# Turned tokens read back by one transfer a tile, and the last block's sums gated earlier

## The chip, the cores and the metric

The kernel runs on one core of a Trainium2 chip. The metric is the device time of one execution in microseconds (us); the kernel before takes 471.35 us, the median of three runs (470.61 to 472.19). The five engines of the core are TensorE (PE; PEld is its weight load), VectorE (DVE), ScalarE (ACT), GpSimd (POOL) and SyncE (SP), which here issues nearly all transfers. Sixteen DMA engines carry the transfers.

## The reference

One transformer-like layer on 2048 tokens of 448 features, conditioned on a vector `c`:

```python
mod = (silu(c) @ w_mod)              # six rows of 448: sa, ca, ga, sb, cb, gb
h = layernorm(x) * (1 + ca) + sa
x = x + ga * ssm_conv(h)             # long convolution along the tokens, plus h * Dskip
h = layernorm(x) * (1 + cb) + sb
x = x + gb * ((silu(h @ w_gate) * (h @ w_up)) @ w_down)   # 448 -> 1792 -> 448
```

## The kernel before

The 2048 tokens are 16 tiles of 128; two tiles make a block, so there are eight blocks. The hidden width 1792 is 14 slices of 128 (`f` = 0 to 13). Per block and slice, TensorE computes gate and up (`gate_up`, 21 steps of contraction 64, the gate's on the upper half of the array and the up's on the lower), VectorE and ScalarE form silu(gate) * up and split it into a high and a low part (`gating`, lines L774 to L792; in the last slice L774, then L781 to L784 in two halves), and TensorE adds the slice's part of the down product to two PSUM banks, `sums` (`point`, called in the middle of a later slice's steps: after the number of steps given by `POINT`). All matrix products are made as three products of high and low parts. The weights are loaded and split in the first block and stay in SBUF.

While TensorE works on block b, the other engines prepare the two tiles of block b + 1: first norm, the convolution (by a short path of triangular products, which lands in the sums of the other PSUM pair), second norm. What is done in which slice is written by hand in `PLANS`: one string for the first block, one for the blocks 1 to 6, one for the last; a `;` ends a slice, a letter is a step and the digit its tile. The steps that matter here:

- `X`, `Y`: second norm, two VectorE operations (L207, L209). A `+` before a name puts the step inside `gating`, after the product silu * up (L786) and ahead of the split into high (L791, ScalarE) and low (L792, VectorE); without it the step follows the gating.
- `T` (`turn`): VectorE transposes the tile in blocks of 32 x 32 (L239), and SP writes it to DRAM (`xd`, L240).
- `U` (`turned_back`): SP reads it back from DRAM into `place[q]` (L245), so that the features stand on the partitions, the 64 features of a chunk twice (both halves of the array need them).
- `split_turned`: at the block's last slice ScalarE (L252) and VectorE (L253) split the turned tokens into `hhi` and `hlo`, chunks 0 to 3 ahead of the last gating and 4 to 6 behind it. TensorE's first products of the next block read these.

In `turned_back` four transfers of 32 partitions each, four runs of 224 numbers a partition, bring a tile back. SP works its list in order: each write, each wait and each read is issued after the one before it.

In the last block nothing is prepared. After slice 13's gating, `last_sums` multiplies the two finished sums (of slices 0 to 11) by the row `gb` (L832) and adds them to `x` (L833), and `finish` computes the down products of slices 12 and 13 (whose weights were multiplied by `gb` before), adds them in three parts (L852) and issues the output transfers.

Of the kernel before, what the change touches and what calls it, by code (L numbers as in the profile page):

```python
# [10 lines left out]
F32 = mybir.dt.float32  # L11
# [3 lines left out]
OP = mybir.AluOpType  # L15
# [3 lines left out]
L, D, N, F = 2048, 448, 256, 1792  # L19
# [4 lines left out]
NF = F // 128  # L24
# [9 lines left out]
PLANS = (  # L34
    """pre: s0 t0 R0 ; mid: f ; g a0 s1 t1 R1 ; b0 G ; r0 h0 ; +v0 a1 c0 ; A0 p0 b1 ; B0 e0 E0 ; r1 h1 u0 w0 M0 ; +v1 X0 Y0 c1 p1 ; A1 T0 ;
    B1 E1 m1 M1 ; U0 X1 Y1 T1 ; U1 e1 ; L0 ; L1""",
    """n0 n1 N ; +l0 a0 b0 k0 ; +l1 k1 r0 h0 ; +v0 a1 b1 c0 ; A0 p0 ; B0 e0 E0 c1 ; r1 h1 m0 M0 p1 ; +v1 X0 Y0 L0 L1 ; A1 T0 U0 ; B1 E1 m1 M1 ; X1 Y1 T1 U1 ; e1 ; ;""",
    "; l0 k0 ; l1 k1",
)
POINT = ([12] + [20] * 12 + [12], [12] + [18] * 12 + [12])  # L40
ORDER = """sf x0 x1 sc m10 se sd m11 m20 m21 m00 m01 sb sa m40 m41 m30 m31 w0 m50 m51 w1 d0 d1 x2 w2 x3 d2"""

PLAN = """t4 pa0 t1 S1 t2 pa1 t3 wi ca gp S20 wr h00 gpc gt h01 mp S21 gac m0 dg gdm mpc k0 a2 t5 sq1 mk gdr h10 cp S3 v00 dga a3 o00
# [8 lines left out]
def f32(ap):  # L52
    return ap.bitcast(F32)
# [3 lines left out]
def tile_kernel(ctx, tc, x, a_re, a_im, b_re, b_im, c_re, c_im, log_dt,  # L57
                wd, wgate_up, states, groups, vecs, dft, idft, out):
    nc = tc.nc
    sy, ve, sc, po, pe = nc.sync, nc.vector, nc.scalar, nc.gpsimd, nc.tensor  # L60
# [5 lines left out]
    dram = ctx.enter_context(tc.tile_pool(name="dram", bufs=1, space=bass.MemoryType.DRAM))  # L66
# [9 lines left out]
    xs = {}  # L76
    xbuf = [const.tile([128, D], F32, name=f"x{q}") for q in range(4)]
    gb = const.tile([128, D], F32)
# [18 lines left out]
    place = [stages_[:, q].rearrange("p k c -> p (k c)") for q in (2, 0)]  # L97
# [13 lines left out]
    def split_d(j, part=None):  # L111
        hi, lo = wp[j]
        if not part:
            sc.copy(hi, wdn[j])
        if part != 0:
            ve.tensor_tensor(lo, wdn[j], f32(hi), op=OP.subtract)

    def split_w(j, part):
        w = raw[j]
        if part == 0:  # L120
            sc.copy(wgu[j][:, 0], w)  # L121
        else:
            ve.tensor_tensor(wgu[j][:, 1], w, f32(wgu[j][:, 0]), op=OP.subtract)  # L123
# [69 lines left out]
    n1, n2 = Norm("a"), Norm("b")  # L193
# [37 lines left out]
        ve.tensor_scalar(i, j, 0.0, None, op0=OP.is_equal)  # L231
        return i

    xd = [dram.tile([128, D], F32, name=f"xd{q}") for q in range(2)]

    def turn(i, q):

        src, dst = h_of(i), v0_of(i)
        ve.transpose(dst.rearrange("p (b k r) -> p k b r", b=2, k=7), src.rearrange("p (k b c) -> p k b c", b=2, k=7))  # L239
        sy.dma_start(xd[q], dst)  # L240

    def turned_back(q):
        for z in range(4):
            b = z % 2
            sy.dma_start(place[q][z * 32:(z + 1) * 32].rearrange("c (a n) -> c a n", a=4),  # L245
                         xd[q][:, b * 224:(b + 1) * 224].rearrange("(a c) n -> c a n", a=4))

    def split_turned(ks):
        for q in range(2):
            src = turned[q].rearrange("p a k r -> p k a r")[:, ks]  # L250
            hi, lo = (h[:, ks, cols(q)].rearrange("p k (a r) -> p k a r", a=4) for h in (hhi, hlo))
            sc.copy(hi, src)  # L252
            ve.tensor_tensor(lo, src, f32(hi), op=OP.subtract)  # L253
# [40 lines left out]
    with tc.tile_pool(name="pre", bufs=1) as pre:  # L294
# [4 lines left out]
        for kind, q in ((n[0], n[1:]) for n in ORDER.split()):  # L299
# [3 lines left out]
            elif kind == "m":  # L303
                g, b = int(q[0]), (slice(0, 2 * D), slice(2 * D, NM))[int(q[1])]
# [36 lines left out]
        for z in range(2):  # L341
# [16 lines left out]
        m0, m0_, a1, a2, m1 = (pre.tile([128, 4], F32, name=q) for q in ("m0", "m0_", "a1", "a2", "m1"))  # L358
# [3 lines left out]
        h01, v0, v1, hd = ([pre.tile([128, w], t, name=f"{n}_{q}") for q in range(2)] for n, t, w in  # L362
                               (("h", F32, D), ("v0", F32, D), ("v1", F32R, D), ("hd", F32, D)))
# [116 lines left out]
        k0, k1 = CV[:, 0:D], DN[2][:, 0:D]  # L480
# [259 lines left out]
    def run_blocks(pools, stages, first=None):  # L740
# [3 lines left out]
        def both(top, low):  # L744

            done = []
            for pair in zip_longest(top, low):
                for e, op in zip(halves, pair):
                    if op:
                        o, w, r, start, stop = op  # L750
                        done.append(pe.matmul(o, w[e], r[e], start=start, stop=stop).ins)  # L751
            return done

        def ffn(b, ts, fresh, last, todo):
            n, sums = 256, SUMS[b % 2]
            pp = {}

            def gate_up(f):
                w, ps = wgu[f], [bank(), bank()]
                prod = [(0, hhi), (1, hhi), (0, hlo)]  # L760
                if fresh and f < NF - 1:
                    order = [(z, k) for z in ((0, 1, 2) if f == 0 else (0, 2, 1)) for k in range(7)]
                else:
                    order = [(z, k) for ks in (LOW, HIGH) for z in range(3) for k in range(7)[ks]]
                ops = [(w[:, prod[z][0], k], prod[z][1][:, k], q == 0, q == 20) for q, (z, k) in enumerate(order)]
                return ps, [[(t[:, 0:n], *o) for t in ps] for o in ops]

            def gating(f, ps, nw):
                p = hid.tile([128, 256], F32, name="p") if fresh else p_of[f % 2]
                hi = hid.tile([128, 256], F32R, name="phi")  # L770
                lo = hid.tile([128, 256], F32R, name="plo")
                for g, a in todo.get(-2, []) if f == 0 else []:
                    g(*a)
                gate_ready[:] = [sc.activation(p, ps[0][:, 0:n], AF.Silu).ins.name]  # L774
                pp[f] = hi, lo
                if f == NF - 1:
                    if fresh:
                        split_d(f, 1)
                    for q in range(3):
                        for o in [cols(q)] * (q < 2):  # L780
                            ve.tensor_tensor(p[:, o], p[:, o], ps[1][:, o], op=OP.mult)  # L781
                            sc.copy(hi[:, o], p[:, o])
                        for o in [cols(q - 1)] * (q > 0):
                            ve.tensor_tensor(lo[:, o], p[:, o], f32(hi[:, o]), op=OP.subtract)  # L784
                    return
                ve.tensor_tensor(ps[1][:, 0:n], p, ps[1][:, 0:n], op=OP.mult)  # L786
                if fresh:
                    split_d(f, 1)
                for g, a in todo.get((f, "+"), []) + todo.get(-1, [])[f * NF:]:
                    g(*a)  # L790
                sc.copy(hi, ps[1][:, 0:n])  # L791
                ve.tensor_tensor(lo, ps[1][:, 0:n], f32(hi), op=OP.subtract)  # L792
                if nw is not None:
                    split_w(nw, 0)
                if fresh:
                    sc.copy(wp[f + 1][0], wdn[f + 1])
# [25 lines left out]
            def gated(f):  # L822

                raw = stage_d[NS - 1]
                sy.dma_start(raw, wd[f * 128:(f + 1) * 128, :])
                po.tensor_tensor(raw, raw, gb, op=OP.mult)
                wdn[f] = raw

            def last_sums():

                for q, i in enumerate(ts):
                    ve.tensor_tensor(sums[q][:, 0:D], sums[q][:, 0:D], gb, op=OP.mult)  # L832
                    ve.tensor_tensor(xs[i], sums[q][:, 0:D], xs[i], op=OP.add)  # L833

            def finish():
                o = [*SUMS[1 - b % 2], bank()]
# [36 lines left out]
            for f in range(NF):  # L873
                ps, ops = gate_up(f)
                ops = list(zip(*ops))
                at = POINT[b > 0][f]
                both(ops[0][:at], ops[1][:at])
                point(f)
                both(ops[0][at:], ops[1][at:])
                if f == NF - 1 and not last:  # L880
                    split_turned(LOW)
                gating(f, ps, f + 2 if fresh and f + 2 < NF else None)
                if f == NF - 1 and not last:
                    split_turned(HIGH)
                if last and f in (2, 5):
                    gated(NF - 2 + (f == 5))
                if last and f in (4, 7):
                    split_d(NF - 2 + (f == 7))
                if last and f == NF - 1:
                    last_sums()  # L890
                    return finish()
                if fresh and f == 0 and first is None:
                    sy.dma_start(run[0:1], run[127:128])
                for g, a in todo.get(f, []):
                    g(*a)
                if fresh:
                    if f + 2 < NF:
                        split_w(f + 2, 1)
                    pools.load(f + 2 + NS, f + NS)
# [4 lines left out]
        if first is not None:  # L904
# [8 lines left out]
            for q, i in enumerate(TILES[0]):  # L913
                t = work.tile([128, 7, 2, 64], F32, name="xn2")
# [156 lines left out]
    for i in TILES[-1]:  # L1071
        c = slice(256 if i + 1 == NT else 0, D)
# [33 lines left out]
def build(nc, aps, out):  # L1106
    with tile.TileContext(nc) as tc:
        a = dict(aps)
        tile_kernel(tc, a["A_u"].rearrange("b l d -> (b l) d"), *[a[n] for n in _INS[1:] + ["B_w_gate_up", "A_states", "w_mod_groups", "c_log_dt", "dft", "idft"]],
                    out.rearrange("b l d -> (b l) d"))  # L1110
# [20 lines left out]
```

## Time and profile before

| | |
|---|---|
| median of three runs | 471.35 us (470.61 to 472.19) |
| the profiled execution's own time | 470.57 us |
| its span (first to last instruction) | 468.8 us |
| mean granted TensorE clock | 0.997 |
| turned tokens written to DRAM (L240) | 14 transfers of 224 KB, median 1.9 us to landing |
| turned tokens read back (L245) | 56 transfers of 112 KB, median 3.1 us to landing |
| gate and up weights loaded (L104) | 14 transfers of 448 KB, median 3.4 us to landing |

The page's first part gives the busy time of each engine and its share of the span. A wait is a line "engine tile line <- engine tile line: us in total, times, longest": who stood idle, and what released it. The chain of waits is followed back from the last instruction: at each step to what released it. A timeline row has the start in us, the duration, engine, line, operation, output<-input, and in brackets the idle time just before. "SPq" is the queue of SyncE: its rows are the issue of a transfer, not the transfer. The DMA view gives, for a stretch, the packets, the megabytes and the share of the sixteen engines' time by queue: q1 is SP's queue, q10 ScalarE's.

### The profile page before, as it was taken

To read this page: it belongs to the slowest core of one execution; us is meant where nothing else is said; L and a number is where in the kernel's file an instruction comes from. 1 tells how busy PE (TensorE), PEld (TensorE's weight loads), DVE (VectorE), ACT (ScalarE), POOL (GpSimd) and SP (SyncE) were. 2 spreads that over 40 slices of the span, in tenths; PEclk is the share of its full clock that TensorE was granted. 3 is DMA by queue.
4 is the path that set the end of the run, shared out by engine and by line. 5 is a ranking of instruction groups with operands and counts; after the bars stand their busy time and mean duration, and the time that the engine had idled before them with its cause. 6 is when DMAs were issued, how large, how long until landed. Compare 5 with 4: busy or idle time off the path is not lost.

```text
span 468.8 us, 14329 instructions
## 1 busy us (share of the span) xinstructions
PE 445.5 (95%) x6271; PEld 422.9 (90%) x6271; DVE 296.0 (63%) x605; ACT 159.8 (34%) x390; POOL 95.6 (20%) x125
## 2 busy tenths in 40 slices
PE   6889998899999999999999999999998999999993
PEld 4558988799999999999998999999998999999993
DVE  4888979865765756565764756565764756543224
ACT  5876564532323222332223232332223232322220
POOL 1235112015200241025100241025100241001000
PEclk9999999999999999999999999999999999999998
DMA  8963555502021202202021202202021102211001
GB/s 303 406 235 100 178 161 174 140 22 82 2 80 42 63 19 60 62 12 70 2 80 43 78 3 60 62 20 63 2 80 42 41 3 60 61 40 44 3 3 45
DMA packets 22408, 35.71 MB, mean 76 GB/s; under 512 B 3008, under 2 KB 18240, under 8 KB 22336
## 3 DMA queue, kind: packets, MB, share of 16 engines
q1 hardware_dynamic: 21696, 34.53, 22.8%
q8 instruction: 51, 0.84, 0.8%
q10 hardware_dynamic: 640, 0.18, 0.2%
q14 instruction: 21, 0.17, 0.1%
HBM read 27.76 MB, written 6.88 MB: 74 GB/s over the span
## 4 chain that ended last, share of the span: by engine, by line
PE 69%; DVE 11%; DMA 7%; ACT 6%; issue 4%; SPq 2%; POOL 1%; DVEq 0%; ACTq 0%; POOLq 0%
PE bank L751 43%; PE dn L751 16%; PE cv L751 8%; DMA raw<-xd 3%; DMA xd<-m 3%; SPq L245 2%; DVE gu L123 2%; DVE bank L786 1%; DVE m L207 1%; DVE m L209 1%; ACT gu L121 1%; DVE m L239 1%; ACT phi L791 1%; ACT hhi L252 1%; DVE plo L792 1%
## 5 line engine op out<-in xcount | busy, mean ns | idle before, releaser
L751 PE MATMUL bank<-hhi,gu 64*128 64x256 f32 x3136 | 225.4, 275 | 7.8 <-DVE gu L123 3.9
L751 PEld LDWEIGHTS bank<-hhi,gu 64*128 64x128 f32 x3136 | 205.3, 184 | 11.3 <-DVE gu L123 5.1
L751 PE MATMUL bank<-hlo,gu 64*128 64x256 f32 x1568 | 131.8, 274 | 0.0
L751 PEld LDWEIGHTS bank<-hlo,gu 64*128 64x128 f32 x1568 | 119.2, 184 | 1.8
L786 DVE TENSOR_TENSOR bank<-raw,bank 128x256 f32<-128x256 f32 x91 | 39.0, 429 | 102.3 <-ACT raw L774 101.7
L774 ACT ACTIVATE raw<-bank 128x256 f32<-128x256 f32 x98 | 37.6, 384 | 188.3 <-PE bank L751 188.3
L751 PE MATMUL dn<-wdh,plo 64*128 64x448 f32 x332 | 84.2, 362 | 1.3 <-DVE plo L792 1.3
L751 PE MATMUL dn<-wdh,phi 64*128 64x448 f32 x332 | 84.2, 360 | 0.3 <-DVE run L727 0.3
L751 PE MATMUL dn<-wdl,phi 64*128 64x448 f32 x332 | 84.0, 360 | 0.0
L792 DVE TENSOR_TENSOR plo<-bank,phi 128x256 fp32r<-128x256 f32 x104 | 44.0, 423 | 29.5 <-ACT phi L791 29.5
L791 ACT CAST phi<-bank 128x256 fp32r<-128x256 f32 x104 | 38.9, 374 | 61.9 <-DVE bank L786 61.9
L751 PEld LDWEIGHTS dn<-wdh,plo 64*128 64x128 f32 x332 | 44.9, 184 | 3.3 <-DVE plo L792 1.8
L751 PEld LDWEIGHTS dn<-wdh,phi 64*128 64x128 f32 x332 | 44.9, 184 | 1.8 <-DVE run L727 0.6
L751 PEld LDWEIGHTS dn<-wdl,phi 64*128 64x128 f32 x332 | 45.0, 184 | 1.0
L751 PE MATMUL cv<-wdh,plo 64*128 64x448 f32 x108 | 38.8, 360 | 0.0
L751 PE MATMUL cv<-wdl,phi 64*128 64x448 f32 x108 | 38.8, 359 | 0.0
L751 PE MATMUL cv<-wdh,phi 64*128 64x448 f32 x108 | 38.6, 358 | 0.0
L183 POOL TENSOR_SCALAR rsa<-mva 128x2 f32<-128x2 f32 (+1 forms) x9 | 3.5, 387 | 112.4 <-DVE mva L155 111.8
L183 POOL TENSOR_SCALAR rsb<-mvb 128x1 f32<-128x1 f32 x16 | 4.3, 266 | 104.0 <-DVE mvb L155 103.4
L253 DVE TENSOR_TENSOR hlo<-raw,hhi 128x512 fp32r<-128x512 f32 (+1 forms) x28 | 16.8, 624 | 11.7 <-ACT hhi L252 10.3
L970 POOL TENSOR_TENSOR m<-m,gm 128x448 f32<-128x448 f32 x12 | 13.9, 1158 | 44.7 <-issue 37.3
L751 PEld LDWEIGHTS cv<-wdh,plo 64*128 64x128 f32 x108 | 19.9, 184 | 0.6
(237 smaller groups left out, 533.5 us busy)
## 6 DMA issues: line engine op xcount, KB each, us to landing
raw<-in_B_w_gate_up_dram SPq DMA_DIRECT2D x14, 448.0 KB, 3.4
raw<-xd SPq DMA_DIRECT2D x56, 112.0 KB, 3.1
rawd<-in_B_w_down_dram SPq DMA_DIRECT2D x16, 224.0 KB, 3.6
xd<-m SPq DMA_DIRECT2D x14, 224.0 KB, 1.9
x<-in_A_u_dram SPq DMA_DIRECT2D x12, 224.0 KB, 3.6
out_dram<-x SPq DMA_DIRECT2D x11, 224.0 KB, 2.5
wm<-in_w_mod_groups_dram SPq DMA_DIRECT2D x5, 448.0 KB, 8.2
wm<-in_w_mod_groups_dram SPq DMA_DIRECT2D x5, 336.0 KB, 8.2
```

What stands on the lines that cost most here:

```text
L121: sc.copy(wgu[j][:, 0], w)
L123: ve.tensor_tensor(wgu[j][:, 1], w, f32(wgu[j][:, 0]), op=OP.subtract)
L183: po.tensor_scalar(rs[:, 0:n], self.mv[:, 0:n, 1], EPS, None, op0=OP.add)
L207: ve.scalar_tensor_tensor(to, xs[i], m, cbw, op0=OP.subtract, op1=OP.mult)
L245: sy.dma_start(place[q][z * 32:(z + 1) * 32].rearrange("c (a n) -> c a n", a=4), xd[q][:, b * 224:(b + 1) * 224].rearrange("(a c) n -> c a ...
L253: ve.tensor_tensor(lo, src, f32(hi), op=OP.subtract)
L751: done.append(pe.matmul(o, w[e], r[e], start=start, stop=stop).ins)
L774: gate_ready[:] = [sc.activation(p, ps[0][:, 0:n], AF.Silu).ins.name]
L786: ve.tensor_tensor(ps[1][:, 0:n], p, ps[1][:, 0:n], op=OP.mult)
L791: sc.copy(hi, ps[1][:, 0:n])
L792: ve.tensor_tensor(lo, ps[1][:, 0:n], f32(hi), op=OP.subtract)
L970: en.tensor_tensor(v, h, g, op=OP.mult)
```

## The change

Four edits:

1. `turn` writes a tile by two transfers instead of one. The DRAM buffer is now 64 rows of 896 numbers, laid out as the features-on-partitions tile will be: feature, then group of 32 tokens, then the 224 numbers of a run. Each transfer has 128 runs of 896 bytes.
2. `turned_back` reads a tile by one transfer instead of four: the 64 rows of 3584 bytes, twice, onto the 128 partitions.
3. In the blocks 1 to 6 the second tile's `X` goes into the gating of its slice (`+X1`).
4. In the last block, slice 13's `point` comes after 8 steps instead of 12, and three of the four operations of `last_sums` (the first tile's two, and the second's multiplication) stand ahead of slice 13's gating; the fourth stays behind it.

```diff
-    """n0 n1 N ; ... ; B1 E1 m1 M1 ; X1 Y1 T1 U1 ; e1 ; ;""",
+    """n0 n1 N ; ... ; B1 E1 m1 M1 ; +X1 Y1 T1 U1 ; e1 ; ;""",
...
-POINT = ([12] + [20] * 12 + [12], [12] + [18] * 12 + [12])
+POINT = ([12] + [20] * 12 + [12], [12] + [18] * 12 + [12], [12] + [18] * 12 + [8])
...
-    xd = [dram.tile([128, D], F32, name=f"xd{q}") for q in range(2)]
+    xd = [dram.tile([64, 2 * D], F32, name=f"xd{q}") for q in range(2)]
...
-        sy.dma_start(xd[q], dst)
+        for k in range(2):
+            sy.dma_start(xd[q][k * 32:(k + 1) * 32].rearrange("c (a n) -> a c n", a=4), dst[:, k * 224:(k + 1) * 224])
...
     def turned_back(q):
-        for z in range(4):
-            b = z % 2
-            sy.dma_start(place[q][z * 32:(z + 1) * 32].rearrange("c (a n) -> c a n", a=4),
-                         xd[q][:, b * 224:(b + 1) * 224].rearrange("(a c) n -> c a n", a=4))
+        sy.dma_start(place[q], xd[q][None].to_broadcast([2, 64, 2 * D]))
...
-            def last_sums():
-
-                for q, i in enumerate(ts):
-                    ve.tensor_tensor(sums[q][:, 0:D], sums[q][:, 0:D], gb, op=OP.mult)
-                    ve.tensor_tensor(xs[i], sums[q][:, 0:D], xs[i], op=OP.add)
+            def last_sums(*parts):
+
+                for q, k in parts:
+                    i, t = ts[q], sums[q][:, 0:D]
+                    if k == 0:
+                        ve.tensor_tensor(t, t, gb, op=OP.mult)
+                    else:
+                        ve.tensor_tensor(xs[i], t, xs[i], op=OP.add)
...
-                at = POINT[b > 0][f]
+                at = POINT[2 if last else b > 0][f]
...
+                if last and f == NF - 1:
+                    last_sums((0, 0), (0, 1), (1, 0))
                 gating(f, ps, f + 2 if fresh and f + 2 < NF else None)
...
                 if last and f == NF - 1:
-                    last_sums()
+                    last_sums((1, 1))
                     return finish()
```

More of the change, by code (lines that the diff above doesn't have):

```diff
@@ L36 @@
     B1 E1 m1 M1 ; U0 X1 Y1 T1 ; U1 e1 ; L0 ; L1""",
-    """n0 n1 N ; +l0 a0 b0 k0 ; +l1 k1 r0 h0 ; +v0 a1 b1 c0 ; A0 p0 ; B0 e0 E0 c1 ; r1 h1 m0 M0 p1 ; +v1 X0 Y0 L0 L1 ; A1 T0 U0 ; B1 E1 m1 M1 ; X1 Y1 T1 U1 ; e1 ; ;""",
+    """n0 n1 N ; +l0 a0 b0 k0 ; +l1 k1 r0 h0 ; +v0 a1 b1 c0 ; A0 p0 ; B0 e0 E0 c1 ; r1 h1 m0 M0 p1 ; +v1 X0 Y0 L0 L1 ; A1 T0 U0 ; B1 E1 m1 M1 ; +X1 Y1 T1 U1 ; e1 ; ;""",
     "; l0 k0 ; l1 k1",
 )
-POINT = ([12] + [20] * 12 + [12], [12] + [18] * 12 + [12])
+POINT = ([12] + [20] * 12 + [12], [12] + [18] * 12 + [12], [12] + [18] * 12 + [8])
 ORDER = """sf x0 x1 sc m10 se sd m11 m20 m21 m00 m01 sb sa m40 m41 m30 m31 w0 m50 m51 w1 d0 d1 x2 w2 x3 d2"""
```

## The prediction

> **What bounds the kernel now.** I read the page's engine line first, then the chain that ended last.
>
> ```profile
> PE 445.5 (95%) x6271; PEld 422.9 (90%) x6271; DVE 296.0 (63%) x605; ACT 159.8 (34%) x390; POOL 95.6 (20%) x125
> ...
> PE 69%; DVE 11%; DMA 7%; ACT 6%; issue 4%; SPq 2%; POOL 1%; DVEq 0%; ACTq 0%; POOLq 0%
> ```
>
> TensorE is the bound. Anything off TensorE counts only where TensorE waits for it. The list of waits says where the turned tokens make it wait:
>
> ```profile
> ACT hhi L252 <- DMA raw<-xd: 10.2, 6, 2.4
> ...
> PE bank L751 <- ACT hhi L252: 3.4, 5, 1.2
> ```
>
> So the transfers that the change touches cost 3.4 us of TensorE's time, in five of the seven block boundaries. No more than that can be won there. The chain around one boundary (between the third and the fourth block) shows how that comes about. Columns: start, duration, what.
>
> ```profile
> 187.82 0.44 DVE bank L786
> ...
> 188.69 0.42 DVE plo L792
> 189.12 0.60 DVE m L207
> ...
> 189.81 0.69 DVE m L209
> ...
> 190.53 0.66 DVE m L239
> ...
> 191.24 1.93 DMA xd<-m
> ...
> 193.23 0.30 SPq L245
> ...
> 194.79 3.04 DMA raw<-xd
> ...
> 197.85 0.63 ACT hhi L252
> ...
> 198.52 1.54 PE bank L751 x21
> ```
>
> The second tile is normalised (L207, L209), turned (L239), written out (1.93 us) and read back by four transfers, from the first issue at 193.23 to the last landing at 197.83: 4.6 us. TensorE resumes at 198.52. The timeline gives what it lost, and the first tile's transfers of the same block (issue start, us in issue):
>
> ```profile
> 182.35 0.33 SPq L240 DMA_DIRECT2D xd<-m  x1
> 184.35 1.75 SPq L245 DMA_DIRECT2D raw<-xd  x4
> ...
> 198.52 1.20 PE L751 MATMUL bank<-hhi,gu 64*128 64x256 f32 x16 [0.34 <-ACT hhi L252]
> ```
>
> So TensorE had run out of work at 198.52 - 0.34 = 198.18. That is this boundary's deadline.
>
> **The earlier normalisation (+X1).** L207 moves from behind the low half L792 to the front of it. It can start at 188.26, when L786 ends, takes 0.68 with its gap, and L792 follows at 188.95 instead of 188.69, ending at 189.37. L209 starts at 189.40, not 189.81: the second tile's write is issued 0.41 us earlier, at 190.83. The low half comes 0.26 us later; it is used only by the next slice's down products, some 3 us on, so that costs nothing.
>
> **The transfers.** Bytes stay: 224 KB out and 448 KB back per tile. Runs change. The write becomes two transfers of 128 runs of 896 bytes, the read one of 128 runs of 3584 bytes. SP issues three transfers in place of five; a write's issue takes 0.33 us, so the second is issued some 0.35 us behind the first, and the read waits for both. What decides is how many of the 16 DMA engines share a transfer. The DMA view over 243 to 252 us (one boundary: one write, four reads, one copied row) and over 10 to 20 us (engines saturated):
>
> ```profile
> DMA  0000008980000009554662100026987300000100
> ...
> q1 hardware_dynamic: 720, 0.69, 26.1%
> ...
> q10 hardware_dynamic: 32, 0.00, 0.3%
> ```
>
> ```profile
> DMA packets 1418, 4.07 MB, mean 407 GB/s; under 512 B 159, under 2 KB 159, under 8 KB 1418
> ```
>
> Five transfers of 128 runs are 640 packets; the other 80 are 16 for each transfer. Every engine closes its own share, so all 16 took part. Even the single row (q10, 3.5 KB) makes 32: 16 pieces and 16 closings, so it was cut into 16 to be spread. In all transfers of this program the outermost step of both sides counts 128, 32 or 16. The new read's source counts 2 outermost (the same 64 rows twice), the new write's target counts 4 (the four groups of 32 tokens). No row shows such a transfer, so the cost has two ends.
>
> *Wide end:* spread over 16 as now. The weight load is the nearest row, same bytes, same runs, same target:
>
> ```profile
> DMA to landing us min/median/max: 3.1/3.4/9.7
> ```
>
> Then both writes land at about 190.83 + 0.35 + 1.93 = 193.1, the read at 196.5, and its split (0.63) ends at 197.2, a microsecond before the deadline. The boundaries' 3.4 us go, and no other wait is near: the split's own products follow in the order of today.
>
> *Narrow end:* the engines share the outermost step, two for the read and four for the writes. Saturated, 16 engines moved 407 GB/s, 25.4 GB/s each: a 3584-byte run takes 0.141 us. Each of two engines gets 64 runs, 9.0 us, where eight runs now take 1.1; with the 2.0 us that the 3.1 of the load hold beside its eight runs, a read takes 11.0 us. Short runs: 26.1% of 16 engines over 9 us for 720 packets is 0.052 us each. Each of four engines gets 32 runs of each of two writes, 3.3 us, where nine packets now take 0.47 of the 1.93: the pair lands 4.8 us after its first issue.
>
> I take the narrow end. In every row the closings equal a divisor of the outermost counts, and the copied row had to be given 16 pieces for it; a scheme blind to the nesting would not need that. The Trainium skill, "DMA: Bandwidth & Descriptors", section "Rules for kernel authors", says it outright: "an outermost dim of size c < 16 — e.g. a leading zero-stride broadcast of c copies — confines the whole DMA to at most c engines". By that rule the sum is the narrow one, 578; without it 465.6; no transfer of this trace has such a dim, so the trace can neither agree nor disagree.
>
> *Working, narrow, at this boundary.* When data begin after an issue:
>
> ```profile
> 243.51 0.34 SPq L240 DMA_DIRECT2D xd<-m  x1
> ```
>
> First tile: write at 182.35, landed 187.15, read issued 187.2; its data run on two engines from 188.05 to 197.05 (data begin 0.84 us after an issue: in the DMA row above, in slices of 0.225 us from 243, the first busy slice starts at 244.35, and the write was issued at 243.51; the rest of the fixed part comes behind the data). Second tile: writes issued at 190.83, but two of their four engines are still at the first tile's read, in the same queue; they finish at 197.05 + 3.33 = 200.4, landed 201.0 (1.93 - 0.84 - 0.47 = 0.62 behind the last run). Read issued 201.05, landed 212.05, split 212.7, TensorE resumes at 212.75 against the deadline of 198.18: 14.6 us. If the queue does not hold the second tile's writes back, they land at 195.65, the read at 206.7, TensorE resumes at 207.4: 9.2 us, the lower bound. At 20.2 GB/s an engine (the page's whole queue below) a run takes 0.177, two reads 4.7 us more in all: the upper bound, 19.3.
>
> ```profile
> q1 hardware_dynamic: 21696, 34.53, 22.8%
> ```
>
> (22.8% of 16 x 468.8 is 1710 us for 34.53 MB.) The other five steady boundaries run the same order of work, and I give them the same price. The first boundary keeps its order (no +X1 there):
>
> ```profile
> 81.92 1.76 SPq L245 DMA_DIRECT2D raw<-xd  x4
> 85.19 0.34 SPq L240 DMA_DIRECT2D xd<-m  x1
> ...
> 93.88 1.07 PE L751 MATMUL bank<-hhi,gu 64*128 64x256 f32 x16
> ```
>
> First read's data 82.8 to 91.8, second writes landed 95.75, read landed 106.8, TensorE resumes at 107.5 instead of 93.88: 13.6 us (7.8 without the queue). Sum: 6 x 14.6 + 13.6 = 101.2, less the 3.4 already paid: 97.8 us.
>
> *Who stands behind the waits.* On ScalarE the split of the second tile stands ahead of the last slice's SiLU, so that slice's gating waits with it, as today. On SP the next transfers are the block's output writes, due two slices later; they are not missed. In the first block a W_down slice's load queues behind the first read on two engines; what it delays falls into the stall.
>
> *TensorE after a pause.* It never pauses over 2 us now, save at the start. There:
>
> ```profile
> 1.52 4.97 PE L291 MATMUL bank<-tri 128*128 128x512 f32 x14 [1.52 <-DVE tri L323]
> ...
> 155.59 1.21 PE dn L751 x12
> ```
>
> In steady state 12 products of 448 columns take 1.21, two at a time, so 512 columns cost 0.23 and 14 of them 3.2; the first ones took 4.97. A pause of 14 us may cost up to those 1.7 us each time: between 0 and 12 for seven; I take 12, the only row of TensorE that starts from rest.
>
> **The end.** The chain there:
>
> ```profile
> 457.73 1.08 PE bank L751 x18
> ...
> 458.86 0.39 ACT raw L774
> ...
> 459.27 0.30 DVE raw L781
> ...
> 459.93 0.49 DVE plo L784 x2
> 460.42 0.56 DVE dn L832
> ...
> 461.00 0.62 DVE x L833
> 461.62 0.55 DVE cv L832
> ...
> 462.20 0.62 DVE x L833
> ...
> 463.27 0.68 DVE x L852 x2
> ```
>
> Three of the four operations L832/L833 move ahead of the last gating. They need the finished sums, which four steps (eight products, 0.46 us) fewer ahead of the point bring to 457.3, and VectorE, which is free at 457.57 (row below). They take 1.76 (460.42 to 462.18), to about 459.4, while SiLU L774 ends at 459.25: the gating slips 0.13. Then one operation of 0.62 and the three additions (1.13): 462.35 instead of 463.95, with TensorE's last product done at 461.51 + 0.13. Gain 1.6 us; at worst the slip takes all 1.76 and 0.1 is left.
>
> ```profile
> 457.15 0.42 DVE L792 TENSOR_TENSOR plo<-bank,phi 128x256 fp32r<-128x256 f32 x1 [0.44 <-ACT phi L791]
> ...
> 461.24 0.27 PE L845 MATMUL bank<-wdh,plo 128*128 128x192 f32 x1
> ```
>
> **Sum.** The profiled execution took 470.57 (span 468.8 and 1.8 around it), 0.8 below the median 471.35. 470.57 + 97.8 + 12 - 1.6 = 578.8; I say 578. Own range: without queue and without the slow start 470.57 + (6 x 9.2 + 7.8 - 3.4) - 1.6 = 528; with slower runs, partly, 600.
>
> **Rivals.**
> *Wide spread:* the engines share the 128 runs however nested. 470.57 - 3.4 - 1.6 = 465.6, faster. For it: the 128 partitions are the outermost count on the other side. Against it: the copied row's 16 pieces. It decides if a read closes with 16 packets, not 2.
> *Narrow writes, wide read:* the pair lands at 4.8 instead of 1.93, 0.41 earlier issued: +2.4; the read takes 3.35 instead of 4.6: -1.25. Six boundaries x 1.15 - 1.6 = +5.3: 475.9, slower.
> *Wide, but the turn isn't worth it:* two writes of short runs and the wait for both eat what the read saves, about 470; same. Against it: a microsecond of slack above.
>
> **Chances.** Narrow read 0.68, narrow writes alone 0.05, wide 0.22, no change 0.05. So slower 0.73, faster 0.22, same 0.05 (0.3%, 1.4 us, is about what tells from no change here: the runs span 470.61 to 472.19). The narrow case's own range leaves out three in ten, so the stated range reaches to the wide case: 464.5 to 600.
>
> **What would show it.** Right: the packets of a boundary's read are 128 + 2, the writes' 128 + 4; the read lands 10 to 12 us after its issue, not 3; the wait of TensorE for the split is 9 to 15 us seven times, also at the first boundary; the DMA share between blocks is 1 to 2 tenths for long. The end: one L833 behind the gating, last addition about 1.6 us nearer to TensorE's last product. Wrong: 16 closings each, a landing near 3.3 us, no TensorE wait for the split, and a time near 465.6.

## The result, and the profile after

The changed kernel takes 587.19 us (median of four runs, 585.71 to 589.51) against 471.34 us: a ratio of 1.246, 95% interval 1.242 to 1.251. The profiled execution took 587.11 us with a span of 585.3, so 116.5 us more span than before. The page of the changed kernel, engine line and chain:

```profile
PE 461.8 (79%) x6271; PEld 441.1 (75%) x6271; DVE 295.0 (50%) x605; ACT 160.2 (27%) x390; POOL 95.6 (16%) x125
...
PE 59%; DMA 27%; DVE 7%; ACT 3%; issue 3%; SPq 1%; POOL 1%; ACTq 0%; DVEq 0%; POOLq 0%
```

TensorE does the same 6271 products. Its share falls from 95% to 79%, and DMA holds 27% of the chain instead of 7%. The waits name the place (us in total, times, longest):

```profile
ACT hhi L250 <- DMA raw<-xd: 108.4, 13, 13.7
...
PE bank L749 <- ACT hhi L250: 107.3, 7, 15.9
```

TensorE's wait for the split (the second line) was 3.4 us in all, in five boundaries; now it is 15.3 on average, in all seven. The chain around the boundary between the third and the fourth block, the one shown before (line numbers are those of the new text: the turned tile's write is L241, its read L244, the split L250):

```profile
225.13 0.66 DVE m L239
...
226.44 9.89 DMA xd<-m
...
236.46 11.41 DMA raw<-xd
...
247.90 0.63 ACT hhi L250
...
248.57 2.93 PE bank L749 x24
```

The write, 1.93 us before, lands 10.5 us after its first issue (225.85); the read, 4.6 us for four transfers before, takes 11.4. SP's issues at that boundary show the first tile's write and read just ahead:

```profile
217.68 1.11 SPq L241 DMA_DIRECT2D xd<-m  x2
222.26 0.54 SPq L244 DMA_DIRECT2D raw<-xd  x1
225.85 1.10 SPq L241 DMA_DIRECT2D xd<-m  x2
```

The DMA view says how many engines took part: first over 218 to 222.2 us, with only the first tile's pair of writes in it, then over 236 to 249, with only the second tile's read:

```profile
q1 hardware_dynamic: 264, 0.23, 17.7%
```

```profile
DMA  0000030011201111111111111111111111100000
...
q1 hardware_dynamic: 130, 0.46, 9.6%
```

The pair of writes makes 264 packets, 2 x (128 + 4); the read 130, 128 + 2. So four engines close a write and two the read (a closing packet is the one that an engine adds behind its share of a transfer), and the row of digits stands at one tenth (two of sixteen) for 8 us. Over 225 to 252 us the view's rate is level at 53 GB/s while the read runs, 26.5 an engine.

The price of the pause is in the windows after TensorE resumes (columns: stretch, us, busy of each engine, granted clock, DMA share, GB/s):

```profile
248.00:250.00 2.00, 1.43 (x12) 1.43 (x14) 1.28 (x4) 1.33 (x5) 0.00 (x0) 0.50 0.00 0
250.00:252.00 2.00, 2.00 (x19) 1.96 (x18) 1.32 (x4) 0.80 (x2) 0.00 (x0) 0.50 0.00 0
252.00:254.00 2.00, 2.00 (x22) 1.84 (x21) 0.00 (x0) 0.00 (x0) 0.00 (x0) 0.72 0.00 0
254.00:256.00 2.00, 2.00 (x40) 2.00 (x40) 0.57 (x2) 0.76 (x2) 0.00 (x0) 1.00 0.04 8
```

TensorE starts at half clock and stays there to about 253.1, some 4.5 us, and loses half of that. At the seven boundaries the half clock lasts 2.9 to 6.1 us, and the granted clock over the 10 us behind each gives 15.3 us lost in all. TensorE's busy time has grown by 16.3 us (445.5 to 461.8); the other 1.2 lie at the start, where its first 14 products took 4.97 us before and now take 6.17:

```profile
1.52 6.17 PE L289 MATMUL bank<-tri 128*128 128x512 f32 x14 [1.52 <-DVE tri L321]
```

They cost the kernel nothing, since the wait for the first weights behind them is 1.3 us shorter.

At the end, the last gating's SiLU starts at 577.50 and the chain closes with

```profile
579.65 0.03 DVE x L853
...
580.19 0.17 DVE x L853
...
580.52 0.35 DVE x L853
```

so 3.37 us from SiLU to last addition, where it was 5.09 (458.86 to 463.95).

### The profile page after: what moved, and what is told of

It reads as the page before. It is cut to its first block, busy times and chain, and to the rows that moved or that the text cites. A ratio compares the mean times of both kernels' runs of the same rounds, so it can differ in the third digit from the quotient of the medians.

```text
span 585.3 us, 14284 instructions
## 1 busy us (share of the span) xinstructions
PE 461.8 (79%) x6271; PEld 441.1 (75%) x6271; DVE 295.0 (50%) x605; ACT 160.2 (27%) x390; POOL 95.6 (16%) x125
## 4 chain that ended last, share of the span: by engine, by line
PE 59%; DMA 27%; DVE 7%; ACT 3%; issue 3%; SPq 1%; POOL 1%; ACTq 0%; DVEq 0%; POOLq 0%
PE bank L749 37%; DMA raw<-xd 14%; PE dn L749 14%; DMA xd<-m 12%; PE cv L749 6%; DVE bank L784 1%; DVE m L207 1%; DVE m L209 1%; DVE gu L123 1%; DVE m L239 1%; ACT hhi L250 1%; SPq L241 1%; DMA vec<-in_c_log_dt_dram 1%; PE dn L481 0%; ACT gu L121 0%
## 5 line engine op out<-in xcount | busy, mean ns | idle before, releaser
L749 PE MATMUL bank<-hhi,gu 64*128 64x256 f32 x3136 | 243.3, 281 | 111.5 <-ACT hhi L250 107.3
L749 PEld LDWEIGHTS bank<-hhi,gu 64*128 64x128 f32 x3136 | 222.5, 190 | 115.3 <-ACT hhi L250 108.7
L749 PE MATMUL bank<-hlo,gu 64*128 64x256 f32 x1568 | 145.6, 279 | 0.0
L749 PEld LDWEIGHTS bank<-hlo,gu 64*128 64x128 f32 x1568 | 133.4, 189 | 0.8
L749 PE MATMUL dn<-wdh,plo 64*128 64x448 f32 x332 | 91.6, 368 | 1.3 <-DVE plo L790 1.3
L749 PE MATMUL dn<-wdh,phi 64*128 64x448 f32 x332 | 92.3, 370 | 0.3 <-DVE run L725 0.3
L749 PE MATMUL dn<-wdl,phi 64*128 64x448 f32 x332 | 91.8, 367 | 0.0
L749 PEld LDWEIGHTS dn<-wdh,phi 64*128 64x128 f32 x332 | 51.2, 192 | 1.5 <-DVE run L725 0.6
L749 PEld LDWEIGHTS dn<-wdl,phi 64*128 64x128 f32 x332 | 51.2, 191 | 0.6
L250 ACT CAST hhi<-raw 128x512 fp32r<-128x512 f32 (+1 forms) x28 | 15.1, 562 | 108.4 <-DMA raw<-xd 108.4
```

## The experiments

Each kernel was timed in turn with the kernel before. The theory that they test: the engines share the outermost step of an access pattern, the queue of a busy engine holds up what comes behind, and TensorE pays once more for the pause. All edits are against the changed kernel unless said otherwise.

**Read by two transfers of 64 rows.**

```diff
-        sy.dma_start(place[q], xd[q][None].to_broadcast([2, 64, 2 * D]))
+        for h in halves:
+            sy.dma_start(place[q][h], xd[q])
```

> The changed kernel, but the read is two transfers of 64 rows, one for each half of the partitions: same bytes, same 3584-byte runs, the outermost step now counts 64. Writes as changed (outermost count 4). Theory (the engines share the outermost step): 16 engines again, each read lands about 3.4 us after its issue instead of 11.4; the write pair still lands about 4.6 us after its first issue. TensorE's wait for the split at a steady boundary 4.6 + 0.1 + 3.75 + 0.65 - 7.35 = 1.7 us instead of 15.3, no half clock: 475 to 477 us. Rival (what is slow is the same 64 rows read twice from DRAM, or long runs of fresh rows, not the count of engines): stays above 560 us.

Measured: 483.33 us, ratio 1.029 (1.024 to 1.033). Same bytes, same runs, same rows read twice: of the 116 us, 104 are gone. The DMA view over 200.1 to 205 us, with one pair of reads in it, has 160 packets, 2 x (64 + 16): sixteen engines close each read.

```profile
q1 hardware_dynamic: 160, 0.46, 34.3%
```

The rival falls: it is the outermost count. The time missed the forecast by 6 us. Its waits:

```profile
PE bank L750 <- ACT hhi L251: 14.7, 7, 2.3
```

That is 2.1 us a boundary, not 1.7, and the first boundary has it too. The second read of a pair is issued 0.5 us behind the first and lands later than I had priced it, 4.2 us after the pair's first issue (200.13) instead of 3.75:

```profile
200.67 3.69 DMA raw<-xd
```

The rest is the clock: the seven pauses are 1.8 to 2.3 us long, and after two of them (2.3 and 2.2 us, the first and the fourth) it drops to half, here behind the first boundary:

```profile
92.00:96.00 4.00, 1.70 (x24) 1.49 (x22) 0.77 (x2) 0.90 (x2) 0.00 (x0) 0.92 0.52 143
96.00:100.00 4.00, 4.00 (x40) 3.90 (x40) 2.80 (x8) 1.33 (x4) 0.00 (x0) 0.65 0.20 57
100.00:104.00 4.00, 4.00 (x66) 3.94 (x64) 2.08 (x5) 0.76 (x2) 0.00 (x0) 1.00 0.01 4
```

**All transfers wide.** The read as above, and the write as four transfers of 32 partitions:

```diff
-        for k in range(2):
-            sy.dma_start(xd[q][k * 32:(k + 1) * 32].rearrange("c (a n) -> a c n", a=4), dst[:, k * 224:(k + 1) * 224])
+        to = xd[q].rearrange("(k c) (a n) -> a c k n", k=2, a=4)
+        for a in range(4):
+            sy.dma_start(to[a], dst[a * 32:(a + 1) * 32].rearrange("p (k n) -> p k n", k=2))
```

> As the run before, and the write is four transfers of 32 partitions (outermost count 32, runs of 896 bytes). Theory: all transfers on 16 engines; the last write is issued 1.1 us behind the first and lands about 3.0 us after it, the read pair 3.75 us after that, against a deadline 7.35 us behind the first write: TensorE waits 0 to 0.4 us a boundary. 465.5 to 468.5 us, faster than the kernel before. Rival (the writes' short runs or the wait for several transfers eat the gain): 470 or more.

Measured: 469.96 us, ratio 0.9985 (0.9967 to 1.0004): no difference from the kernel before that can be told. It is 1.5 us above the expected range. Narrow writes alone, beside wide reads, cost 13 us (483.3 to 470.0). The chain of the same boundary:

```profile
190.74 0.31 SPq L242
...
192.03 1.69 DMA xd<-m
...
193.79 0.45 SPq L246
194.28 4.00 DMA raw<-xd
```

Four issues make the write 3.0 us long instead of 1.93, and the pair of reads takes 4.5 us, as long as the four short-run reads before (4.6). From the first issue of the reads to the split, the six steady boundaries average 4.6 us here and 4.6 in the kernel before (4.1 with the wide reads and narrow writes), so runs four times as long bought half a microsecond at most. The weight load's 3.1 to 3.4 us, by which I had priced them, is not what these reads take. TensorE's wait is 5.2 us in all, more than the 3.4 of before, and that eats most of what the other two edits give.

**The old transfers, the other edits kept.**

```diff
-    xd = [dram.tile([64, 2 * D], F32, name=f"xd{q}") for q in range(2)]
+    xd = [dram.tile([128, D], F32, name=f"xd{q}") for q in range(2)]
...
-        for k in range(2):
-            sy.dma_start(xd[q][k * 32:(k + 1) * 32].rearrange("c (a n) -> a c n", a=4), dst[:, k * 224:(k + 1) * 224])
+        sy.dma_start(xd[q], dst)
...
-        sy.dma_start(place[q], xd[q][None].to_broadcast([2, 64, 2 * D]))
+        for z in range(4):
+            ...
```

> The changed kernel with the transfers of before (one write, four reads, DRAM buffer as before): the earlier normalisation and the last block's edits alone. Theory: the normalisation takes 0.41 us off each steady boundary's wait, 1.8 of the 3.4 us in all, the end gives 1.7: 467.5 to 468.5 us. Rival (both are hidden and only the transfers matter): 471.

Measured: 464.34 us, ratio 0.986 (0.984 to 0.989), faster than both kernels, and 3 us below the range that I expected. Behind the transfers stands a gain of 7 us. The next two runs take it apart.

**The last block's edits alone, on the kernel before.**

```diff
-                at = POINT[b > 0][f]
+                at = POINT[2 if last else b > 0][f]
...
+                if last and f == NF - 1:
+                    last_sums((0, 0), (0, 1), (1, 0))
...
-                    last_sums()
+                    last_sums((1, 1))
```

> The kernel before with the last block's edits alone (three of four sums operations ahead of the last gating, the point after 8 steps). Theory: the last addition ends 1.6 to 1.8 us nearer to the last gating's SiLU (5.09 us in the kernel before, 3.3 expected): 469.2 to 470.0 us. Rival (the gating is pushed back by as much as the sums are early): 471.

Measured: 467.73 us, ratio 0.9934 (0.9916 to 0.9952): 3.5 us, twice the forecast. From SiLU (459.09) to the end of the last addition (462.00 + 0.35) it takes 3.26 us, so 1.8 of the gain is the expected one. The rest lies behind it: the span ends 3.85 us after the last addition, not 4.85. The last output transfer lands 2.7 us after its issue; in the kernel before it is 3.8:

```profile
out_dram<-x SPq DMA_DIRECT2D x1, 96.0 KB, 3.8
```

Why is open: bytes and order are the same. From the end of the last addition to the end of the span, the two kernels without the edit have 4.84 and 4.85 us, the eight with it 3.85 to 4.81 (4.43 in the changed kernel, 4.81 in the run below that keeps TensorE busy). So the edit alone does not bring the early landing, and that part of the 3.5 us is not shown to be its gain.

**The earlier normalisation alone, on the kernel before.**

```diff
-... ; B1 E1 m1 M1 ; X1 Y1 T1 U1 ; e1 ; ;
+... ; B1 E1 m1 M1 ; +X1 Y1 T1 U1 ; e1 ; ;
```

> The kernel before with the earlier normalisation alone (+X1). Theory: the second tile's write is issued 0.41 us earlier at six boundaries and TensorE's wait for the split falls from 3.4 us in all to 0.7 to 1.6: 468.5 to 469.8 us. Rival (the reads' landing does not follow the write, the wait stays): 471.

Measured: 467.49 us, ratio 0.9921 (0.9904 to 0.9937), 3.7 us. TensorE's wait for the split falls from 3.4 to 0.3:

```profile
PE bank L751 <- ACT hhi L252: 0.3, 1, 0.3
```

The forecast had left 0.7 to 1.6. SP's issue of the four reads took 2.2 to 3.3 us at the steady boundaries before, and takes 1.73 at five of the six now, 2.78 at one. The boundary that was shown:

```profile
192.83 1.73 SPq L245 DMA_DIRECT2D raw<-xd  x4
```

But a shorter issue was not an earlier landing: only between the fourth and the fifth block does the split start sooner behind the first of the four issues (5.3 us before, 4.8 now); at the other five it took 4.3 to 4.7 us and now takes 4.5 to 5.0. What gave more than 0.41 us a boundary, and what stretched the issues before, is open.

**Only the second tile's read narrow.**

```diff
-        sy.dma_start(place[q], xd[q][None].to_broadcast([2, 64, 2 * D]))
+        if q == 0:
+            for h in halves:
+                sy.dma_start(place[q][h], xd[q])
+        else:
+            sy.dma_start(place[q], xd[q][None].to_broadcast([2, 64, 2 * D]))
```

> The changed kernel, but the first tile's read is two wide transfers; only the second tile's read is the single transfer with outermost count 2. Theory (the second tile's writes stand behind the first tile's read on two engines, in the same queue): now they land 4.6 us after their first issue instead of about 10.5, and TensorE's wait falls from 15.3 to 4.6 + 0.1 + 11.4 + 0.65 - 7.35 = 9.4 us at six boundaries and about 8 at the first, with the half clock after it as long as in the changed kernel: about 546 us (540 to 552). Rival (the queue holds nothing back, the long write landing has another cause): the wait stays at 15 and the time at 580 to 587.

Measured: 544.47 us, ratio 1.157 (1.154 to 1.160). TensorE's wait:

```profile
PE bank L753 <- ACT hhi L254: 64.7, 7, 9.8
```

The second tile's issues at one boundary:

```profile
212.67 1.16 SPq L241 DMA_DIRECT2D xd<-m  x2
217.53 0.54 SPq L248 DMA_DIRECT2D raw<-xd  x1
```

The write pair now lands 4.8 us after its first issue, not 10.5, the narrow read itself still takes 11.2. So it is shown that the first tile's read held the second tile's writes back, by some 5.7 us, 43 us of the total. The trace of the changed kernel shows the order too. From 230.5 to 233.25 us every packet of SP's queue is one of the read's, of 3584 bytes; from 233.5 on every one is a short one of the writes. The DMA view over 231 to 231.5, then over 234 to 235:

```profile
DMA packets 8, 0.03 MB, mean 57 GB/s; under 512 B 0, under 2 KB 0, under 8 KB 8
...
DMA packets 54, 0.05 MB, mean 47 GB/s; under 512 B 2, under 2 KB 54, under 8 KB 54
```

So the two shared engines did not take turns between the transfers; they finished the read first.

**TensorE kept busy through the wait.**

```diff
                 both(ops[0][at:], ops[1][at:])
+                if f == NF - 1 and not last:
+                    for _ in range(62):
+                        pe.matmul(SUMS[1 - b % 2][0].rearrange("p (a b) -> p a b", a=4), tri,
+                                  tri[:, None, :].to_broadcast([128, 4, 128]), start=True, stop=True)
```

> The changed kernel with 62 extra products of 512 columns (into a sums bank that is free then; about 0.23 us each, 14.2 us) behind each of the first seven blocks' last products, so that TensorE works while it waits for the turned tokens; nothing reads them. Theory (after a pause of 15 us TensorE runs 4.6 us at half clock, 2.3 us lost seven times): no slice at half clock, 16 us less than the changed kernel: 570 to 573 us, mean granted clock 0.99 or more. Rival (the half clock is tied to something else, such as the transfers, or costs nothing because other engines bound that stretch): 586 to 588.

Measured: 571.13 us, 16 us under the changed kernel, mean granted clock 0.997. The half clock after the pause is real time, and it is the pause of TensorE that brings it: the transfers are as narrow as before. Work that nobody needs made the kernel faster.

**The whole turn ahead of the low half,** with the old transfers and the last block's edits.

```diff
-... ; B1 E1 m1 M1 ; +X1 Y1 T1 U1 ; e1 ; ;
+... ; B1 E1 m1 M1 ; +X1 +Y1 +T1 U1 ; e1 ; ;
```

> The transfers of before, the last block's edits, and the second tile's whole second norm and turn (X1, Y1, T1) ahead of the low half, not X1 alone. Theory: the write goes another 0.4 us earlier, the last of the wait (0.7 us) goes, the low half comes 1.6 us later but 1 us before its use: 463.3 to 464.3 us, at most a tenth of a percent below the kernel with the old transfers (464.3). Rival (the late low half holds TensorE's down products): 465 to 470.

Measured: 466.62 us, ratio 0.991 (0.989 to 0.993), 2.3 us slower than with X1 alone ahead. The rival was right: TensorE's wait for the split (0.7 us with X1 alone) is gone, and the one for the low half has grown from 1.3 us:

```profile
PE dn L751 <- DVE plo L792: 3.5, 7, 1.3
```

The two waits account for 1.5 of the 2.3 us; the two profiled executions differ by 1.3.

## Why the prediction was right

*The spread, which decided.* Forecast 128 + 2 and 128 + 4 packets; 130 and 264 measured. No row of before had an outermost count below 16, so the choice rested on the shape of the rows there and on the rule that the prediction cites. The rule of the Trainium skill ("DMA: Bandwidth & Descriptors", "Rules for kernel authors") holds here to the packet, and the run with 64 outermost rows shows it from the other side: 16 closings a read.

*The sizes.* A read took 11.4 us (forecast 11.0), an undisturbed pair of writes 4.6 (217.68 to 222.26; forecast 4.8), the pair behind the first tile's read 10.5 (forecast 201.0 - 190.83 = 10.2), a steady boundary's wait 14.9 to 15.9 (forecast 14.6). Together the waits gave 107.3 us where 101.2 were forecast. The undisturbed writes were priced a little high, the rest a few per cent low, and the issue of these transfers takes 0.54 us, not the 0.33 taken from the rows before. The first boundary was the furthest off: 15.3 where 13.6 was forecast, since its second writes landed 11.8 us after their first issue (forecast 10.6) and its read took 11.6.

*The pause.* I took 1.7 us a boundary from the kernel's first products and bounded it by zero; at the seven boundaries it is 1.4 to 3.0, 15.3 in all where 12 was forecast. For its size, that term was the one furthest off, and that it came this near is partly luck. The row it was taken from does not show a half clock: the profile grants 1.00 there, and the same 14 products took 6.17 us in the changed kernel. By that row the price would have been 6.17 - 3.2 = 3.0 and not 1.7. The half clock lasted 2.9 to 6.1 us behind a pause of 15, 4.4 on average. The Trainium skill, "TensorE: Matmul & The Clock Gate", Part 1, gives at least one busy window of about 3.4 us before full clock comes back, and says that the windows run freely, so that the moment varies. This trace agrees on average and in that it varies, though one boundary, with 2.9, stays under that window.

*The end.* Forecast 1.6, measured 5.09 - 3.37 = 1.7.

*Sum.* 107.3 - 3.4 + 15.3 - 1.7 = 117.5 against 116.5 of span. Of the rest, 0.4 is the last output, which lands that much sooner behind the last addition; 0.6 is not traced. The forecast 578 is 9 us under the measured time: 6 of it in the waits, 3 in the clock.

*Where it was off without consequence.* The rival "wide spread" was priced at 465.6 with the weight load's landing; with everything wide it came to 470.0, with six transfers a tile in place of the rival's three: a pair of reads took 4.5 us and not 3.4, the writes 3.0 and not 2.3. That is no gain over the old transfers. And the two small edits were worth 7 us, not 5, with about one of the 7 in the last output's landing, whose cause is open.

## What to carry to other kernels

Look at the outermost count on both sides of a transfer before its run length: here a 2 in place of a 32 made a tile's read 11.4 us instead of 4.6, and a 4 in place of a 128 made its write 4.6 instead of 1.93, while runs four times as long were worth half a microsecond at most. One slow transfer costs more than its own time, since what follows in the same queue waits on the same engines, and TensorE came back at half clock from every pause of 9 to 16 us here. Test the parts of a bundled change apart: two edits that together came to 1.4% stood in this one under a loss of 25%.

## What the runs showed of the hardware

After pauses of TensorE of 2.3 and 2.2 us the clock stood at half at two of seven boundaries, and after five others of 1.8 to 2.3 us it did not; what chose the two was not found. The time that SP takes to issue a transfer differed with its shape: 0.33 us for the write of 224 KB from 128 partitions, some 0.54 for each of the turned tokens' transfers in the changed kernel (112 and 448 KB). The last output landed up to a microsecond sooner in most kernels with the last block's edits, but hardly so in the one that kept TensorE busy, and no cause was found.
